# Interleaving GpSimd's minima, a new balance of two engines' accounts, and another order of the last two steps in a top-32 attention and squared-ReLU kernel

## Chip, cores and metric

The kernel runs on one core of a Trainium2 chip. The metric is device microseconds of one execution, the median over several. Before the change it is 874.69 us (three runs, 873.51 to 876.08).

The engines are named as the profile names them: PE is TensorE (PEld its weight loads), DVE is VectorE, ACT is ScalarE, POOL is GpSimd, SP is SyncE, which here only starts DMAs.

## The reference

Attention in which each row of scores keeps its 32 largest, then a two-layer network with a squared ReLU:

```python
# q, k, v: (8, 8, 576, 64) float32; w_in: (512, 2048); w_out: (2048, 512)
scores = scale * np.matmul(q, k.transpose(0, 1, 3, 2))
kth = np.partition(scores, -top_k, axis=-1)[..., -top_k:-top_k + 1]     # top_k = 32
scores = np.where(scores >= kth, scores, -1000000000.0)
attn = np.exp(scores - np.max(scores, axis=-1, keepdims=True))
attn = attn / (np.sum(attn, axis=-1, keepdims=True) + 1e-09)
x = np.matmul(attn, v).transpose(0, 2, 1, 3).reshape(4608, 512)
h = np.maximum(x @ w_in, 0.0)
out = h * h @ w_out
```

## The kernel before

**Steps.** The work is 144 steps (U), each two tiles of 128 score rows by 576 columns: 64 (batch, head) pairs, nine tiles per two heads. A step's two tiles lie side by side as `[:, 2, 576]`. The program's order is written out by hand (each instruction goes through `pin`, which keeps program order), so each engine has one queue in that order. The loop for steps 0 to 124 (Z = 125) comes first, then a second loop to step 141, then steps 142 and 143 written out, with the end of the network.

**A step's way.** For step w: `scores` (L202) has PE fill two PSUM banks sc_a and sc_b with halves of 288 columns, and ScalarE copies both into `s` (L207). `split` (L235 to 240) has VectorE take the larger of each column of one half and its partner in the other, into `tops`. `bring` (L223) has PE copy half of the tops into a free part of sc_b, called `far`. `join` (L250) has VectorE compare the two halves of tops again: the larger of each pair goes to the first 144 columns of `cat`, the smaller to the next 144. `small_mins` (L263, L264) has GpSimd put the smaller of each first pair into the last columns of cat. So cat holds the row's 576 values, sorted a little, and `topk` (L282, L286) takes 8 values from it four times, from 100, 120, 256 and 576 columns: MAX8, then MATCH_REPLACE8 to strike out what was found. The joint minima (columns 144 to 288) are first read by the third round, the small ones by the fourth.

[...]

Then `below` (L328) and `expo` (L337) have ScalarE make a mark for each score under the 32nd and the exponentials, `mask` (L333) has GpSimd combine them, `turn` (L376) transposes the weights by a DMA on SP's queue, `products` (L404) has PE multiply them by the values, `invert` (L409, L415) has VectorE take the reciprocals of the sums, and `place` (L432, L437) has ScalarE write the rows of x. A finished block of x goes through the network in pieces: `ups` (L506, with ReLU on ScalarE at L512 and the square on GpSimd at L520 or on ScalarE at L517) and `downs` (L534, out by L544 or L542).

**The accounts.** `debt` holds how far GpSimd (G) and ScalarE (A) are behind in microseconds, as the program reckons: each step takes away 5.8 and 6.0 (`pass_step`), each piece of work adds its price (`owe`). Three choices follow from it. A split is *lent* (all 288 smaller values on GpSimd, not 144) where G is under 4.9. A step is *joint* where its split is lent and G is under 4.5 (5.5 near the end): then VectorE leaves out the second operation of `join`, and GpSimd makes these minima in `joint_mins` (L256, L257). A square goes to ScalarE where A is under 5.4 and G over 5.0.

**The order around it.** In step u the small minima are those of step u + 2 (of u + 1 up to step 11), the joint ones those of u + 1, the mask is that of u - 1. GpSimd's queue in a step of the long run is:

```python
        if lead > 1:
            joint_mins(u + 1)
        if u == DEEP + 2:
            small_mins(u + 2)
        elif u != DEEP + 1:
            small_mins(u + lead)
```

and later in the step `mask(u - 1)`, with squares, casts of v (L154) and a small check (`note`) in between.

**The end.** Steps 142 and 143 fill x's last block. `x_last` (L871, L873) transposes a quarter of it on PE and copies it on ScalarE, `ups_last` (L878) multiplies that quarter by w_in into sc_a and sc_b, `square_last` (L883, L885) squares, and the last downs (L951) end the kernel. `expo_last` (L366) and `mask_last` (L371) do the last step's exponentials on ScalarE and its mask on VectorE; `turn_last` (L386 to 391) transposes on PE.

Of the kernel before, what the change touches and what calls it, by code (L numbers as in the profile page):

```python
# [22 lines left out]
def kernel(  # L23
# [34 lines left out]
    def pass_step(more=0.0):  # L58
        for e in debt:
            debt[e] = max(0.0, debt[e] - {"G": 5.8, "A": 6.0}[e] - more)  # L60

# [182 lines left out]
    def join(u):  # L244
        d = st[u]
        d["joint"] = "lent" in d and DEEP + 4 <= u < U - 6 and debt["G"] < (4.5 if u < Z + 2 else 5.5)
        if d["joint"]:
            owe(G=1.6)
        for lo, op in ((0, ALU.max), (QUAR, ALU.min))[0:1 if d["joint"] else 2]:
            pin(nc.vector.tensor_tensor(d["cat"][:, :, lo:lo + QUAR], far, d["tops"][:, :, 0:QUAR], op=op))  # L250

    def joint_mins(u):
        d = st[u]
        if d["joint"]:
            at, tops = d["cat"][:, :, QUAR:HALF].bitcast(i32), d["tops"][:, :, :].bitcast(i32)
            pin(nc.gpsimd.tensor_tensor(at, tops[:, :, 0:QUAR], tops[:, :, QUAR:HALF], op=ALU.add))  # L256
            pin(nc.gpsimd.tensor_tensor(at, at, d["cat"][:, :, 0:QUAR].bitcast(i32), op=ALU.subtract))  # L257

    def small_mins(u):
        d = st[u]  # L260
        n = HALF if "lent" in d else QUAR
        s, at = d["s"], d["cat"][:, :, HALF:HALF + n].bitcast(i32)
        pin(nc.gpsimd.tensor_tensor(at, s[:, :, 0:n].bitcast(i32), s[:, :, HALF:HALF + n].bitcast(i32), op=ALU.add))  # L263
        pin(nc.gpsimd.tensor_tensor(at, at, d["tops"][:, :, 0:n].bitcast(i32), op=ALU.subtract))  # L264

# [65 lines left out]
    def mask(u):  # L331
        w = w_two[u % 3][:, :, 0:S].bitcast(i32)
        pin(nc.gpsimd.tensor_tensor(w, w, marks[u % 2][:, :, :].bitcast(i32), op=ALU.add))  # L333

    def expo(u, x):
# [312 lines left out]
    join(0)  # L648
    small_mins(0)
    scores(1)  # L650
# [22 lines left out]
    for u in range(Z):  # L673
# [3 lines left out]
        pass_step()  # L677
        owe(A=4.5 if u < DEEP + 15 else 4.12, G=3.0)
        if u > 0:
# [21 lines left out]
        if checks:  # L701
            note()
        if lead > 1:
            joint_mins(u + 1)
        if u == DEEP + 2:
            small_mins(u + 2)
        elif u != DEEP + 1:
            small_mins(u + lead)
        dense(u, 0)
        if u and not DEEP < u < DEEP + 3:  # L710
            bring(u + lead)
        if u > 0:
            below(u - 1, 1)
            topk(u, (1,))
            if u == DEEP + 1:
                join(u + 1)
            topk(u, (2,))
            if u == DEEP + 1:
                split(u + 2)
                small_mins(u + 2)  # L720
                ahead(u + 3)
                bring(u + 2)
            topk(u, (3,))
            if u == DEEP:
                join(u + 1)
                split(u + 2)
            elif u != DEEP + 1:
                join(u + 2 if u > DEEP else u + 1)
            exps(u - 1)
            mask(u - 1)  # L730
            turn(u - 1)
# [12 lines left out]
        if u == DEEP:  # L744
            small_mins(u + 2)
            ahead(u + 3)
            bring(u + 2)
# [18 lines left out]
    for u in range(Z, U - 2):  # L766
        now[0] = u
        pass_step(0.3)
        owe(A=4.12, G=3.0)
        below(u - 1, 0)  # L770
# [9 lines left out]
        if checks:  # L780
            note()
        joint_mins(u + 1)
        small_mins(u + 2)
        if u == U - 8:
# [64 lines left out]
    topk(u, (2,), lambda: invert(u - 2))  # L849
    place(u - 2)  # L850
    topk(u, (3,))
    w = w_two[u % 3]
    for x in range(2):
        below(u, x)
        at = w[:, x, 0:S].bitcast(i32)
        pin(nc.gpsimd.tensor_tensor(at, at, marks[u % 2][:, x, :].bitcast(i32), op=ALU.add))
    turn(u)
    flush()
    square()
# [15 lines left out]
    def up_last(hp, f0, khs):  # L875
        for kh in khs:
            for n in range(4):
                pin(nc.tensor.matmul(out=hp[:, n * 128:(n + 1) * 128], lhsT=w_in[:, kh, (f0 + n) * 128:(f0 + n + 1) * 128],  # L878
                                     rhs=xl[:, kh, :], start=False, stop=(kh == KH - 2 and n == 3)))

# [16 lines left out]

    x_last((0,))
    hold["out"] = True
    u = U - 1  # L900
    topk(u, (0, 1))
    expo_last(0)
    expo_last(1)
    products(u - 2)
    downs.pop(0)()
    downs.pop(0)()
    topk(u, (2,), lambda: invert(u - 2))
    place(u - 2)
    topk(u, (3,))
    mask_last(0)  # L910
    mask_last(1)
    ups_last(one, 0)
    turn_last(0)
    ups_last(two, 0)
    x_last((1,))
    turn_last(1)
    ups_last(one, 1)
    st[u]["o"] = ps_one.tile([128, 512], f32, name="gen", bufs=2)[:, 0:130].rearrange("p (x d) -> p x d", x=2)
    products(u)
    verify(u)  # L920
    ups_last(two, 1)
    invert(u)
    place_last(u)
    note()
    downs.pop(0)()
    products(u - 1)
    x_last((3,))
    invert(u - 1)
    place(u - 1)
    downs.pop(0)()  # L930
    flush()
    pin(nc.vector.tensor_reduce(worst[:, 0:1], flags[:, :, 0:OLD], axis=mybir.AxisListType.XY, op=ALU.max))
    ups_last(one, 3)
    ups_last(two, 3)
    x_last((2,))
    sums_checked(nc.vector, OLD, 2 * U)
    pin(nc.vector.tensor_reduce(worst[:, 1:2], flags[:, :, OLD:2 * U], axis=mybir.AxisListType.XY, op=ALU.max))
    pin(nc.vector.tensor_scalar(worst[:, 0:1], worst[:, 0:1], scalar1=worst[:, 1:2], scalar2=0.0, op0=ALU.max, op1=ALU.is_gt))
    for z, bank in ((0, one), (2, two)):
        ups_last(bank, 2)  # L940
        for j in range(2):
# [143 lines left out]
```

## Time and profile before

| what | value |
|---|---|
| median of three runs | 874.69 us |
| the profiled execution | 875.31 us |
| its span on the core | 873.3 us |
| VectorE's share of busy time | 96% |
| ScalarE's | 93% |
| GpSimd's | 90% |
| TensorE's | 87% |
| granted TensorE clock, mean | 0.987 |

The span is what the profiler's records cover; 2.0 us of the execution's time lie around it. Times in rows of a timeline are from the span's start. A timeline row is: start, length, engine, line, operation, output and inputs by the program's names, count, and in brackets the idle time of the engine just before and what ended it. A row of the waits is: who waited for whom, total us, times, longest. A row of the groups is: line, engine, operation, shapes, count, then busy us and mean ns of one, then idle us before them. Rows of consecutive equal operations are merged, with their count. Ends of one operation and starts of the next overlap, so the distance between starts is the time that an operation takes of its engine.

### The profile page before, as it was taken

The numbers are of one execution on the slowest core, as the hardware profiler recorded it, in microseconds if no ns is written. First come the engines' busy times: TensorE is split into PE (matmuls) and PEld (weight loads), VectorE is DVE, ScalarE is ACT, GpSimd is POOL, SyncE is SP. The second block draws the span as 40 slices with busy tenths as digits, with TensorE's granted clock in tenths as the row PEclk, the third lists the DMA queues.
The fourth block names the chain that finished last, engine by engine and source line by source line (L and its number), as shares of the span: only waits on it lengthen the run. The fifth ranks groups of instructions, "written<-read, shape, count | busy, mean of one in ns | idle before, by whom it ended". The sixth has DMA issues, their size and how long they took to land.

```text
span 873.3 us, 19891 instructions
## 1 busy us (share of the span) xinstructions
PE 756.2 (87%) x5948; PEld 483.0 (55%) x6030; DVE 842.3 (96%) x3445; ACT 809.6 (93%) x1630; POOL 787.6 (90%) x722
## 2 busy tenths in 40 slices
PE   6998997888888988889888888898898998999976
PEld 3554555555555554555555555555655654666644
DVE  5999999999999999999999999999999999999994
ACT  2888999899999998999999999999999999999973
POOL 3688999999999999999999999999999998999751
PEclk7999999999999999999999999999999999999999
DMA  5597776545555556456655555665565555433342
GB/s 122 122 226 158 177 180 107 111 93 116 92 122 112 113 111 123 80 113 108 117 109 103 101 111 108 114 126 109 120 119 112 114 102 110 85 69 75 81 75 43
DMA packets 325442, 98.04 MB, mean 112 GB/s; under 512 B 317520, under 2 KB 317776, under 8 KB 325328
## 3 DMA queue, kind: packets, MB, share of 16 engines
q1 hardware_dynamic: 323984, 96.28, 55.5%
q8 instruction: 49, 0.80, 0.4%
q14 instruction: 65, 0.53, 0.2%
q10 hardware_dynamic: 1344, 0.43, 0.2%
HBM read 36.70 MB, written 9.44 MB: 53 GB/s over the span
## 4 chain that ended last, share of the span: by engine, by line
DVE 68%; PE 11%; issue 8%; ACT 7%; POOL 4%; DMA 1%; SPq 0%; DVEq 0%; ACTq 0%; POOLq 0%
DVE m L282 29%; DVE cat L286 21%; DVE tops L235 8%; DVE cat L250 7%; ACT s L207 2%; PE dn_ps L534 2%; PE gen L506 2%; PE sc_b L223 2%; PE sc_b L202 2%; PE av_ps L404 1%; POOL cat L263 1%; PE sc_a L202 1%; PE dn_ps L556 1%; ACT marks_a L328 1%; ACT marks_b L328 1%
## 5 line engine op out<-in xcount | busy, mean ns | idle before, releaser
L282 DVE MAX8 m<-cat 128x8 f32<-128x100 f32 (+3 forms) x1152 | 435.5, 420 | 0.0
L286 DVE MATCH_REPLACE8 cat<-m,cat 128x100 f32<-128x100 f32 (+2 forms) x864 | 259.5, 308 | 0.2
L264 POOL TENSOR_TENSOR cat<-cat,tops 128x576 int32<-128x576 int32 (+1 forms) x144 | 195.1, 1355 | 14.3 <-DVE tops L238 2.5
L263 POOL TENSOR_TENSOR cat<-s 128x576 int32<-128x576 int32 (+1 forms) x144 | 195.2, 1355 | 8.6 <-ACT s L207 7.6
L202 PE MATMUL sc_b<-qkT 64*128 64x288 f32 (+1 forms) x640 | 119.0, 452 | 44.9 <-DVE cat L250 34.5
L534 PE MATMUL dn_ps<-w_out,h 128*128 128x512 bf16 x492 | 132.9, 384 | 10.7 <-ACT wide L544 4.3
L506 PE MATMUL gen<-xT,w_in 128*128 128x256 bf16 (+1 forms) x1088 | 129.3, 265 | 1.1 <-ACT xT L466 0.7
L223 PE MATMUL sc_b<-tops,id_f 128*128 128x144 f32 x524 | 95.5, 305 | 39.5 <-ACT s L207 38.9
L506 PEld LDWEIGHTS <-w_in 128*128 128x128 bf16 x1344 | 110.2, 98 | 32.6 <-issue 19.5
L404 PEld LDWEIGHTS <-wT 128*128 128x128 bf16 (+3 forms) x1600 | 98.0, 99 | 48.1 <-issue 9.0
L223 PEld LDWEIGHTS sc_b<-tops,id_f 128*128 128x128 f32 x524 | 73.5, 190 | 80.2 <-ACT s L207 76.2
L328 ACT ACTIVATE marks_a<-s,m 128x576 bf16<-128x576 f32 x144 | 116.1, 811 | 0.0
L207 ACT ACTIVATE s<-sc_b 128x576 f32<-128x576 f32 x144 | 94.9, 659 | 18.1 <-PE sc_b L202 7.1
L202 PE MATMUL sc_a<-qkT 64*128 64x288 f32 (+1 forms) x640 | 110.9, 428 | 0.9 <-DVE tops L235 0.9
L328 ACT ACTIVATE marks_b<-s,m 128x576 bf16<-128x576 f32 x142 | 110.6, 784 | 0.0
L207 ACT ACTIVATE s<-sc_a 128x576 f32<-128x576 f32 x144 | 95.9, 666 | 6.5 <-PE sc_a L202 3.5
L235 DVE TENSOR_TENSOR tops<-sc_a,s 128x576 f32<-128x576 f32 x131 | 97.8, 747 | 0.0
L250 DVE TENSOR_TENSOR cat<-sc_b,tops 128x288 f32<-128x288 f32 x207 | 86.6, 444 | 4.6 <-PE sc_b L223 4.2
L202 PEld LDWEIGHTS sc_b<-qkT 64*128 64x128 f32 (+1 forms) x640 | 47.9, 176 | 74.1 <-DVE cat L250 45.1
L534 PEld LDWEIGHTS <-h 128*128 128x128 bf16 x560 | 48.0, 98 | 72.2 <-issue 34.4
L512 ACT ACTIVATE rl<-gen 128x512 f32<-128x512 f32 x140 | 84.0, 601 | 1.5 <-PE gen L506 1.5
L202 PEld LDWEIGHTS sc_a<-qkT 64*128 64x128 f32 (+1 forms) x640 | 55.2, 178 | 36.0 <-DVE tops L235 22.2
(133 smaller groups left out, 1348.7 us busy)
## 6 DMA issues: line engine op xcount, KB each, us to landing
out_dram<-wide SPq DMA_DIRECT2D x31, 256.0 KB, 2.6
q_raw<-in_q_dram SPq DMA_DIRECT2D x30, 256.0 KB, 3.7
k_raw<-in_k_dram SPq DMA_DIRECT2D x30, 256.0 KB, 3.8
h<-in_moe_w_in_dram SPq DMA_DIRECT2D x8, 512.0 KB, 5.1
h<-in_moe_w_out_dram SPq DMA_DIRECT2D x8, 512.0 KB, 4.4
v_raw_a<-in_v_dram SPq DMA_DIRECT2D x15, 256.0 KB, 4.0
v_raw_b<-in_v_dram SPq DMA_DIRECT2D x15, 256.0 KB, 3.9
out_dram<-wide SPq DMA_DIRECT2D x9, 128.0 KB, 2.4
```

Source lines behind the costliest of these rows:

```text
L202: pin(nc.tensor.matmul(out=sc[j][r if rest else slice(0, 128), x, 0:HALF], lhsT=qkT[r, 0, c * 128:min(S, (c + 1) * 128)], rhs=qkT[r, 1, j ...
L207: pin(nc.scalar.activation(s[:, :, j * HALF:(j + 1) * HALF], sc[j][:, :, 0:HALF], AF.Copy))
L223: pin(nc.tensor.matmul(out=far[:, x, :], lhsT=id_f[:, :], rhs=st[w]["tops"][:, x, QUAR:HALF], start=True, stop=True))
L235: pin(tt(tops[:, :, :], one, two, op=ALU.max))
L250: pin(nc.vector.tensor_tensor(d["cat"][:, :, lo:lo + QUAR], far, d["tops"][:, :, 0:QUAR], op=op))
L263: pin(nc.gpsimd.tensor_tensor(at, s[:, :, 0:n].bitcast(i32), s[:, :, HALF:HALF + n].bitcast(i32), op=ALU.add))
L264: pin(nc.gpsimd.tensor_tensor(at, at, d["tops"][:, :, 0:n].bitcast(i32), op=ALU.subtract))
L282: pin(nc.vector.max(out=m[r][:, x, :], in_=cat[:, x, at]))
L286: pin(nc.vector.match_replace(out=cat[:, x, at], in_to_replace=m[r][:, x, :], in_values=cat[:, x, at], imm_value=NEG))
L328: pin(nc.scalar.activation(marks[u % 2][:, x, :], d["s"][:, x, :], AF.Relu, bias=d["m"][3][:, x, 7:8], scale=-1.0))
L506: pin(nc.tensor.matmul(out=hp[:, n * n_rows:(n + 1) * n_rows], lhsT=w_in[:, kh, (f0 + n) * 128:(f0 + n + 1) * 128], rhs=xt(kh), start=(kh ...
L534: pin(nc.tensor.matmul(out=op[:, :], lhsT=held["h2"][:, f, c * 128:(c + 1) * 128], rhs=w_out[:, f, :], start=(f == 0), stop=(f == NF - 1)))
```

## The change

It has three parts.

1. `mins` takes the place of `small_mins` and `joint_mins` in the order. With a joint step it emits joint add, small add, joint subtract, small subtract. Without one it emits the small add and puts the subtract off (`put_off`) until just after the next `mask` (`catch_up`), in steps 0 and 1 until just after the add.
2. The accounts: 5.74 instead of 5.8 is taken off G each step, a step's own work is put down at 2.92 instead of 3.0, a joint step at 1.5 instead of 1.6, and a step is joint up to a debt of 4.9 instead of 4.5.
3. The last two steps: `place(u - 2)` of step 142 moves behind `turn(u)`; in step 143 a down piece and the products of step 141 go first, the first `x_last` later, the quarters of x in the order 0, 1, 2, 3 instead of 0, 1, 3, 2, and one reduction of the check's flags (L932) earlier.

```diff
-            debt[e] = max(0.0, debt[e] - {"G": 5.8, "A": 6.0}[e] - more)
+            debt[e] = max(0.0, debt[e] - {"G": 5.74, "A": 6.0}[e] - more)
...
-        d["joint"] = "lent" in d and DEEP + 4 <= u < U - 6 and debt["G"] < (4.5 if u < Z + 2 else 5.5)
+        d["joint"] = "lent" in d and DEEP + 4 <= u < U - 6 and debt["G"] < (4.9 if u < Z + 2 else 5.5)
         if d["joint"]:
-            owe(G=1.6)
+            owe(G=1.5)
...
+    def less(at, a, b, top):
+        add = lambda: pin(nc.gpsimd.tensor_tensor(at, a, b, op=ALU.add))
+        take = lambda: pin(nc.gpsimd.tensor_tensor(at, at, top, op=ALU.subtract))
+        return add, take
+
     def joint_mins(u):
         d = st[u]
-        if d["joint"]:
-            at, tops = d["cat"][:, :, QUAR:HALF].bitcast(i32), d["tops"][:, :, :].bitcast(i32)
-            pin(nc.gpsimd.tensor_tensor(at, tops[:, :, 0:QUAR], tops[:, :, QUAR:HALF], op=ALU.add))
-            pin(nc.gpsimd.tensor_tensor(at, at, d["cat"][:, :, 0:QUAR].bitcast(i32), op=ALU.subtract))
+        at, tops = d["cat"][:, :, QUAR:HALF].bitcast(i32), d["tops"][:, :, :].bitcast(i32)
+        return less(at, tops[:, :, 0:QUAR], tops[:, :, QUAR:HALF], d["cat"][:, :, 0:QUAR].bitcast(i32))
...
-        s, at = d["s"], d["cat"][:, :, HALF:HALF + n].bitcast(i32)
-        pin(nc.gpsimd.tensor_tensor(at, s[:, :, 0:n].bitcast(i32), s[:, :, HALF:HALF + n].bitcast(i32), op=ALU.add))
-        pin(nc.gpsimd.tensor_tensor(at, at, d["tops"][:, :, 0:n].bitcast(i32), op=ALU.subtract))
+        s, at = d["s"][:, :, :].bitcast(i32), d["cat"][:, :, HALF:HALF + n].bitcast(i32)
+        return less(at, s[:, :, 0:n], s[:, :, HALF:HALF + n], d["tops"][:, :, 0:n].bitcast(i32))
+
+    put_off = []
+
+    def catch_up():
+        while put_off:
+            put_off.pop(0)()
+
+    def mins(w):
+        add, take = small_mins(w)
+        if st[w - 1].get("joint"):
+            first, last = joint_mins(w - 1)
+            first()
+            add()
+            last()
+            take()
+        else:
+            add()
+            put_off.append(take)
...
         pin(nc.gpsimd.tensor_tensor(w, w, marks[u % 2][:, :, :].bitcast(i32), op=ALU.add))
+        catch_up()
...
-        owe(A=4.5 if u < DEEP + 15 else 4.12, G=3.0)
+        owe(A=4.5 if u < DEEP + 15 else 4.12, G=2.92)
...
-        if lead > 1:
-            joint_mins(u + 1)
         if u == DEEP + 2:
-            small_mins(u + 2)
+            mins(u + 2)
         elif u != DEEP + 1:
-            small_mins(u + lead)
+            mins(u + lead)
+        if u < 2:
+            catch_up()
...
-        owe(A=4.12, G=3.0)
+        owe(A=4.12, G=2.92)
...
-        joint_mins(u + 1)
-        small_mins(u + 2)
+        mins(u + 2)
...
     topk(u, (2,), lambda: invert(u - 2))
-    place(u - 2)
     topk(u, (3,))
...
     turn(u)
+    place(u - 2)
     flush()
...
-                                     rhs=xl[:, kh, :], start=False, stop=(kh == KH - 2 and n == 3)))
+                                     rhs=xl[:, kh, :], start=False, stop=(kh == KH - 1 and n == 3)))
...
-    x_last((0,))
     hold["out"] = True
     u = U - 1
+    downs.pop(0)()
+    products(u - 2)
     topk(u, (0, 1))
     expo_last(0)
     expo_last(1)
-    products(u - 2)
     downs.pop(0)()
-    downs.pop(0)()
+    x_last((0,))
     topk(u, (2,), lambda: invert(u - 2))
     place(u - 2)
     topk(u, (3,))
     mask_last(0)
     mask_last(1)
+    pin(nc.vector.tensor_reduce(worst[:, 0:1], flags[:, :, 0:OLD], axis=mybir.AxisListType.XY, op=ALU.max))
     ups_last(one, 0)
+    ups_last(two, 0)
     turn_last(0)
-    ups_last(two, 0)
     x_last((1,))
+    downs.pop(0)()
+    products(u - 1)
     turn_last(1)
     ups_last(one, 1)
+    invert(u - 1)
+    place(u - 1)
...
     products(u)
     verify(u)
     ups_last(two, 1)
+    x_last((2,))
     invert(u)
     place_last(u)
     note()
     downs.pop(0)()
-    products(u - 1)
     x_last((3,))
-    invert(u - 1)
-    place(u - 1)
-    downs.pop(0)()
     flush()
-    pin(nc.vector.tensor_reduce(worst[:, 0:1], flags[:, :, 0:OLD], axis=mybir.AxisListType.XY, op=ALU.max))
-    ups_last(one, 3)
-    ups_last(two, 3)
-    x_last((2,))
+    ups_last(one, 2)
+    ups_last(two, 2)
...
-        ups_last(bank, 2)
+        ups_last(bank, 3)
```

More of the change, by code (lines that the diff above doesn't have):

```diff
@@ L648 @@
     join(0)
-    small_mins(0)
+    for go in small_mins(0):
+        go()
     scores(1)
@@ L744 @@
         if u == DEEP:
-            small_mins(u + 2)
+            mins(u + 2)
             ahead(u + 3)
@@ L781 @@
             note()
-        joint_mins(u + 1)
-        small_mins(u + 2)
+        mins(u + 2)
         if u == U - 8:
```

## The prediction

> **What bounds the kernel now.** I read the page's busy shares and its chain, then windows of the steady part, then who waits for whom there.
>
> ```profile
> span 873.3 us, 19891 instructions
> PE 756.2 (87%) x5948; PEld 483.0 (55%) x6030; DVE 842.3 (96%) x3445; ACT 809.6 (93%) x1630; POOL 787.6 (90%) x722
> ...
> DVE 68%; PE 11%; issue 8%; ACT 7%; POOL 4%; DMA 1%; SPq 0%; DVEq 0%; ACTq 0%; POOLq 0%
> ```
>
> The chain runs through VectorE for 68% of the span. The windows below cover steps 28 to 123 or so; their columns are PE, PEld, DVE, ACT and POOL busy time.
>
> ```profile
> 182.00:338.00 156.00, 133.95 (x1065) 85.66 (x1075) 155.88 (x645) 150.47 (x305) 151.90 (x137) 1.00 0.56 109
> 338.00:540.00 202.00, 174.13 (x1393) 112.71 (x1412) 202.00 (x827) 200.37 (x407) 196.74 (x176) 1.00 0.57 111
> 540.00:735.00 195.00, 172.78 (x1368) 112.19 (x1384) 194.36 (x799) 192.90 (x394) 186.49 (x164) 1.00 0.59 113
> ```
>
> VectorE is busy for 202.00 of 202 us in the middle one, so time taken off it there is time off the kernel, as far as the others can follow. They stand close behind: ScalarE is busy for 200.37 us and GpSimd for 196.74. From 186 to 735 us ScalarE waits this often, and VectorE, from 100 to 735 us, once:
>
> ```profile
> ACT s L207 <- DVE cat L286: 2.3, 2, 1.3
> ACT s L207 <- DVE m L282: 1.9, 3, 1.3
> ACT s L207 <- PE sc_a L202: 1.6, 6, 0.3
> ACT qkT L138 <- PE gen L134: 1.1, 5, 0.4
> ...
> DVE cat L250 <- PE sc_b L223: 0.2, 1, 0.2
> ```
>
> ScalarE has 6.9 us of waiting in that stretch, 4.2 of it on VectorE. That is all the time by which it can follow a faster VectorE; beyond it ScalarE sets the pace.
>
> **The joint minima.** Each count here comes from adding up the two debts through the 144 steps with the listing's constants. The old ones give 81 joint steps, 131 lent splits, 95 squares on ScalarE and 45 on GpSimd, which are the counts of the rows:
>
> ```profile
> L256 POOL TENSOR_TENSOR cat<-tops 128x288 int32<-128x288 int32 x81 | 64.8, 800 | 0.0
> L257 POOL TENSOR_TENSOR cat<-cat 128x288 int32<-128x288 int32 x81 | 64.5, 796 | 6.4
> L264 POOL TENSOR_TENSOR cat<-cat,tops 128x576 int32<-128x576 int32 x131 | 184.8, 1411 | 11.0 <-DVE tops L235 0.8
> L520 POOL TENSOR_TENSOR h<-rl 128x512 bf16<-128x512 f32 x45 | 46.6, 1042 | 1.1 <-ACT rl L512 1.1
> ...
> L250 DVE TENSOR_TENSOR cat<-sc_b,tops 128x288 f32<-128x288 f32 x207 | 86.6, 444 | 4.6 <-PE sc_b L223 4.2
> L517 ACT ACTIVATE h<-rl 128x512 bf16<-128x512 f32 x95 | 60.8, 640 | 0.0
> ```
>
> The new constants give 95 joint steps (16, 30, 35, 42, 48, 51, 60, 66, 78, 88, 102, 107, 114, 119 and 122 become joint, 120 no longer is, 128 and 137 take the places of 131 and 136), the same 131 lent splits, 98 squares on ScalarE and 42 on GpSimd. So VectorE loses 14 of its 207 L250 operations, and GpSimd gains 28 operations like L256 and L257. What each takes is the distance from its start to the next one's start, since ends overlap:
>
> ```profile
> 435.60 0.80 POOL L256 TENSOR_TENSOR cat<-tops 128x288 int32<-128x288 int32 x1
> 436.48 0.80 POOL L257 TENSOR_TENSOR cat<-cat 128x288 int32<-128x288 int32 x1
> 436.61 0.80 DVE L250 TENSOR_TENSOR cat<-sc_b,tops 128x288 f32<-128x288 f32 x2
> 437.24 1.41 POOL L263 TENSOR_TENSOR cat<-s 128x576 int32<-128x576 int32 x1
> 437.33 0.75 DVE L235 TENSOR_TENSOR tops<-sc_a,s 128x576 f32<-128x576 f32 x1
> 438.72 1.41 POOL L264 TENSOR_TENSOR cat<-cat,tops 128x576 int32<-128x576 int32 x1
> 439.25 0.67 ACT L517 ACTIVATE h<-rl 128x512 bf16<-128x512 f32 x1
> 439.77 0.69 ACT L207 ACTIVATE s<-sc_b 128x576 f32<-128x576 f32 x1
> 440.09 1.41 POOL L333 TENSOR_TENSOR w_two_c<-w_two_c,marks_b 128x576 int32<-128x576 int32 x1
> ```
>
> VectorE: two L250 in 0.72 us, one is 0.36, so 14 x 0.36 = **5.0 us** off the bounding engine. This is the top of the main term.
>
> GpSimd: L256 to L257, which reads what L256 just wrote, is 0.88 us; L257 to L263, which doesn't, is 0.76. Likewise 1.48 against 1.37. So a dependent pair pays 0.12 us, and in the new order (joint add, small add, joint subtract, small subtract; or add, mask, subtract) no operation follows the one it reads. That takes 0.12 from 144 small and 81 joint pairs: 27.0 us. The 14 new joints cost 14 x 2 x 0.76 = 21.3, three fewer squares save 3 x 1.04 = 3.1. Net, GpSimd has 8.8 us less to do, and its side of the bargain holds.
>
> **What comes late by it.** In a joint step the joint subtract now stands behind the small add, 1.37 us, less the 0.12 saved. Its reader is the 256-wide MAX8 of the next step; the narrowest place is step 91:
>
> ```profile
> 531.68 0.76 PE L223 MATMUL sc_b<-tops,id_f 128*128 128x144 f32 x4 [1.41 <-ACT s L207]
> 532.81 0.45 DVE L250 TENSOR_TENSOR cat<-sc_b,tops 128x288 f32<-128x288 f32 x1
> ...
> 538.93 0.80 POOL L257 TENSOR_TENSOR cat<-cat 128x288 int32<-128x288 int32 x1
> 541.55 0.74 DVE L282 MAX8 m<-cat 128x8 f32<-128x256 f32 x2
> ```
>
> The subtract ends at 539.73, its reader starts at 541.55: 1.82 us, of which about 0.6 stay. In a step without a joint, the mask (L333) runs 1.37 + 0.12 us earlier than now, with the put-off subtract queued behind it; where ScalarE's exponentials aren't ready, GpSimd stands at the mask and everything behind it (that subtract, squares, the next adds) moves back. The subtract itself has time: its first reader is the 576-wide MAX8 two steps on (one, up to step 11). I price both waits at 0 to 0.8 us for VectorE, inside the main term.
>
> ScalarE is what I trust least. Its squares move: six go to it (steps 33, 46, 49, 50, 61, 105), three leave (82, 94, 134), at 439.77 - 439.25 = 0.52 us each. Four of them, 2.1 us, fall in steps 33 to 50. From its 6.9 us of waiting stay 4.8 for following VectorE; if the 2.7 on PE can't be squeezed, 2.1. How ScalarE holds VectorE shows in the rows above: after its copies of s, PE brings the far tops (L223, ended 532.44) and VectorE's join starts at 532.81, a margin of 0.37 us. So the main term lies between 2.1 + 0.36 (step 16, before the stretch) = 2.5 and 5.0. I take **3.3**, a third of the way up, because ScalarE in 338 to 540 us is nearer to full than to having room.
>
> **The tail.** The first x column's transposes and copy leave the head of the last step; a down piece and the products of step U-3 take their place; later ones are put in order 0, 1, 2, 3; the two placing copies of step U-4 go behind the two `below` and the transpose DMA of U-2, which starts some 0.4 us sooner on SP's queue, where nothing waits for it.
>
> ```profile
> 849.60 1.43 ACT L328 ACTIVATE marks_a<-s,m 128x576 bf16<-128x576 f32 x2
> 851.57 0.22 PE L871 MATMUL gen<-id_h,x_tok 128*128 128x128 bf16 x1 [2.25 <-ACT rl L512]
> 851.62 0.78 PE L404 MATMUL av_ps<-vau_f,wT 128*128 128x65 bf16 x10
> 851.95 2.04 POOL L520 TENSOR_TENSOR h<-rl 128x512 bf16<-128x512 f32 x2
> 852.36 1.44 ACT L366 ACTIVATE marks_b<-s,low 128x576 bf16<-128x576 f32 x2
> 852.86 0.17 DVE L409 RECIPROCAL shares<-av_ps 128x2 f32<-128x2 f32 x1 [1.97 <-PE av_ps L404]
> 854.29 1.53 DVE L371 SCALAR_TENSOR_TENSOR w_two_c<-s,m,marks_b 128x576 bf16<-128x576 f32 x2
> 862.27 0.61 PE L878 MATMUL sc_a<-xT,w_in 128*128 128x128 bf16 x8 [0.37 <-ACT xT L873]
> ```
>
> Now PE stands 2.25 us before L871 with the products (L404) queued behind it, and VectorE waits 1.97 us for these. Both waits go. But the first up product then needs the x copy that ScalarE makes after its two L366, which end at 853.80 anyway, so what is late next is ScalarE. The term lies between 0 and 1.97 + 0.37 = 2.3 us; I take **0.7**, nearer to the low end because of that ScalarE row: the 0.37 before the last ups, now covered by other ups, and some 0.3 of better order. The early `worst` reduction and the stop flags I put at nothing: the reduction runs while PE does ups; uncovered, it would cost under 1 us.
>
> A rule of the Trainium skill speaks against this part. VectorE's L371 starts 0.3 us after GpSimd's squares (L520) have ended at 853.99; moved up by VectorE's 1.97 us it would run beside them. SBUF — State Buffer, "Who interferes with whom", says that a VectorE instruction with two SBUF inputs contends with a GpSimd one that reads SBUF, and that the later one is blocked until the first is done. L371 has two such inputs. No row of this trace shows the two at once. By the rule up to one square, 1.04 us, would come back and the sum below would be some 872; by the rows it is 871.
>
> **Sum.** The profiled execution took 875.31 us, 873.3 of span and 2.0 around it: 875.31 - 3.3 - 0.7 = 871.3. It lies 0.6 above the median of the three runs, 874.69, and from that the same terms give 870.7. I forecast **871.0**.
>
> **Rivals.**
> - Full price: ScalarE and GpSimd follow all the way, the tail's waits go for half their worth: 874.7 - 5.0 - 1.0 = 868.7. For it: VectorE waits only 0.2 us in 635 now. Against it: ScalarE's 4.8 us of room must all be found where VectorE needs it.
> - Held: ScalarE's waits on PE stay, GpSimd stands at the earlier masks, and joint subtracts come late by the 0.8; the tail gives nothing: 874.7 - 2.5 + 0.8 = 873.0. For it: the margins of 0.37 and 0.6 us. Against: GpSimd has 8.8 us less work.
> - Slower, because the change doesn't do what it says: the 0.12 us belongs to the operation itself and not to reading a fresh result, so it stays. Then GpSimd has 14 x (0.88 + 0.76) - 3.1 = 19.8 us more. Its idle time in the three windows is 17.9 us, of which some 13 are such gaps (6.4/81 and 11.0/131 are 0.08 us each of idle time, in some 160 pairs), so about 5 are free; its joint subtracts then hold VectorE by about 13 us: 875.3 + 13 - 0.7 = 887. It decides where less than 15/225 = 0.07 of the 0.12 us goes. Against it: L264 followed by L333, equal work on other data, has no gap.
>
> **How the numbers follow.** Forecast 0.50, full price 0.17, held 0.23, slower 0.10. A measurement of this kernel tells about 0.3% from no change, 2.6 us, which is also the spread of the runs shown. The forecast's own range is 870 to 872.5, nearly all faster; with full price that makes 0.62 faster. Held and the forecast's edge make 0.26 within. The slower rival, and what ScalarE could lose beyond it, make 0.12. The range from 868.7 to 874.2 takes in full price and held, and leaves out the slower rival and a tail above or below.
>
> **What would show it.** Right: L250 x193, L256 and L257 x95; 0.76 and 1.37 us between starts inside the four; VectorE still above 99% in 182 to 735 us; steps without an L250 pair 0.36 shorter; no 2.25 at L871. Wrong: MAX8 of 256 waiting for GpSimd L257's successor (the joint subtract came late), L250 waiting for PE by microseconds and ScalarE without waits (ScalarE set the pace), or dependent spacing unchanged (the slower rival).

## The result, and the profile after

The changed kernel takes 879.85 us, median of 8 runs (878.02 to 882.97), against 875.25 us for the kernel before, also 8 runs, the three known before the change among them: ratio **1.0054 [1.0040, 1.0068]**, 0.54% slower. The forecast was 871.0 us, faster.

The page's head of the changed kernel, its span, busy shares and chain:

```profile
span 877.1 us, 19916 instructions
PE 761.5 (87%) x5948; PEld 482.3 (55%) x6030; DVE 839.0 (96%) x3431; ACT 811.4 (93%) x1633; POOL 795.3 (91%) x747
...
DVE 57%; issue 12%; POOL 11%; PE 10%; ACT 7%; DMA 2%; SPq 0%; POOLq 0%; ACTq 0%; DVEq 0%
```

VectorE has 3.3 us less to do and yet the span is 3.8 us longer. In the chain VectorE fell from 68% to 57% and GpSimd rose from 4% to 11%: work on GpSimd now ends some of the waits that count. The same three windows as before the change (PE, PEld, DVE, ACT, POOL):

```profile
182.00:338.00 156.00, 136.40 (x1063) 86.49 (x1078) 154.27 (x634) 151.88 (x309) 153.70 (x143) 0.99 0.60 109
338.00:540.00 202.00, 174.94 (x1390) 112.24 (x1406) 200.07 (x827) 199.81 (x407) 198.65 (x180) 1.00 0.57 109
540.00:735.00 195.00, 170.83 (x1344) 109.55 (x1362) 190.68 (x778) 190.25 (x386) 188.59 (x174) 1.00 0.58 112
```

VectorE idles 1.73, 1.93 and 4.32 us in them, where it idled 0.12, 0.00 and 0.64. Who it waits for, from 100 to 735 us (total, times, longest), where before there was a single 0.2 us:

```profile
DVE cat L306 <- POOL cat L254: 8.2, 18, 0.9
```

L306 is the strike of the rounds (the old L286: one instruction loads the eight values that were found, the next overwrites them). GpSimd makes a minimum out of an integer add and a subtract of the larger value; L253 is the add and L254 the subtract, for joint and small minima alike (the old L256, L263 and L257, L264). So VectorE, about to strike out the first eight values, stands until GpSimd has subtracted. The groups show that the kernel otherwise is what was planned:

```profile
L250 DVE TENSOR_TENSOR cat<-sc_b,tops 128x288 f32<-128x288 f32 x193 | 81.3, 442 | 3.5 <-PE sc_b L223 3.1
L306 DVE MATCH_VALUE_LOAD cat<-m,cat 128x8 f32 x864 | 68.1, 79 | 8.8 <-POOL cat L254 8.2
L253 POOL TENSOR_TENSOR cat<-tops 128x288 int32<-128x288 int32 x95 | 76.2, 802 | 0.0
L254 POOL TENSOR_TENSOR cat<-cat 128x288 int32<-128x288 int32 x95 | 76.0, 800 | 0.0
L254 POOL TENSOR_TENSOR cat<-cat,tops 128x576 int32<-128x576 int32 x131 | 185.1, 1413 | 0.0
L541 POOL TENSOR_TENSOR h<-rl 128x512 bf16<-128x512 f32 x42 | 43.5, 1044 | 0.2 <-ACT rl L533 0.2
```

There are 193 L250, 95 joint pairs and 42 squares on GpSimd, and its subtracts no longer have idle time ahead of them (6.4 and 11.0 us before).

**The place.** Step 91, the narrowest in the prediction. First the kernel before, its VectorE at the same place (the joint subtract there starts at 538.93 and ends at 539.73, a row of the prediction):

```profile
539.70 0.42 DVE L282 MAX8 m<-cat 128x8 f32<-128x100 f32 x2
540.06 0.09 DVE L286 MATCH_VALUE_LOAD cat<-m,cat 128x8 f32 x1
540.14 0.25 DVE L286 MATCH_REPLACE8 cat<-m,cat 128x100 f32<-128x100 f32 x1
```

and the changed kernel, by time over GpSimd and VectorE:

```profile
540.78 0.80 POOL L253 TENSOR_TENSOR cat<-tops 128x288 int32<-128x288 int32 x1
541.53 1.41 POOL L253 TENSOR_TENSOR cat<-s 128x576 int32<-128x576 int32 x1
542.41 0.42 DVE L302 MAX8 m<-cat 128x8 f32<-128x100 f32 x2
542.90 0.79 POOL L254 TENSOR_TENSOR cat<-cat 128x288 int32<-128x288 int32 x1
543.65 1.40 POOL L254 TENSOR_TENSOR cat<-cat,tops 128x576 int32<-128x576 int32 x1
543.72 0.09 DVE L306 MATCH_VALUE_LOAD cat<-m,cat 128x8 f32 x1 [0.89 <-POOL cat L254]
543.80 0.24 DVE L306 MATCH_REPLACE8 cat<-m,cat 128x100 f32<-128x100 f32 x1
```

The joint subtract reads the larger ones of the pairs, `cat[:, :, 0:QUAR]`, 144 wide. The first round strikes in the first 100 of these. It is a write over something still to be read, and it comes 1.49 us sooner than the reader of the subtract's result (540.06 against 541.55). Before, it had 540.06 - 539.73 = 0.33 us to spare. The new order puts the joint subtract 1.37 - 0.12 = 1.25 us later, so 0.92 of wait was to come; the row says 0.89.

**Where the difference arises.** Follow the start of each step's first MAX8 (100 wide), changed kernel minus the kernel before, each counted from its own first one: +1.0 us at step 20, +1.2 at 60, +2.4 at 80, +3.9 at 100, +5.3 at 120. The starts of step 142, the last but one, in the kernel before and then in the changed one:

```profile
842.46 0.41 DVE L282 MAX8 m<-cat 128x8 f32<-128x100 f32 x2
```

```profile
848.11 0.41 DVE L302 MAX8 m<-cat 128x8 f32<-128x100 f32 x2
```

Up to there 5.65 us were lost; the spans differ by 3.8, so the tail gave 1.85 back. Inside the loop 14 x 0.36 = 5.0 us came off VectorE (for most new joint steps, the loop step that holds the shorter join is 0.36 to 0.37 us shorter). The named waits took 8.2. What is left, some 2.5, isn't assigned to single waits.

**GpSimd** also stands more. Its largest waits from 100 to 735 us, the kernel before and then the changed one:

```profile
POOL w_two_a L333 <- ACT w_two_a L337: 2.4, 4, 0.9
POOL w_two_c L333 <- ACT w_two_c L337: 1.8, 5, 0.6
POOL h L520 <- ACT rl L512: 1.1, 1, 1.1
POOL w_two_b L333 <- ACT w_two_b L337: 0.2, 1, 0.2
```

```profile
POOL w_two_b L353 <- ACT w_two_b L358: 8.9, 7, 3.5
POOL w_two_c L353 <- ACT w_two_c L358: 5.0, 5, 1.5
POOL w_two_a L353 <- ACT w_two_a L358: 1.4, 4, 0.8
```

L353 is the mask (old L333), which now comes ahead of the put-off subtract and stands for ScalarE's exponentials: 15.3 us instead of 4.4. What is queued behind it, the next step's joint minima among it, waits with it. The order in time suggests that this is in good part an effect of the strike waits: of the 17 waits at a mask in this stretch, 11 begin 4.2 to 5.3 us after a wait at the strike, and no strike wait has a mask wait in the 6 us before it. So where VectorE was held, GpSimd later stands too, and has less time left to catch up.

### The profile page after: what moved, and what is told of

It reads as the page before. It is cut to its first block, busy times and chain, and to the rows that moved or that the text cites. A ratio compares the mean times of both kernels' runs of the same rounds, so it can differ in the third digit from the quotient of the medians.

```text
span 877.1 us, 19916 instructions
## 1 busy us (share of the span) xinstructions
PE 761.5 (87%) x5948; PEld 482.3 (55%) x6030; DVE 839.0 (96%) x3431; ACT 811.4 (93%) x1633; POOL 795.3 (91%) x747
## 4 chain that ended last, share of the span: by engine, by line
DVE 57%; issue 12%; POOL 11%; PE 10%; ACT 7%; DMA 2%; SPq 0%; POOLq 0%; ACTq 0%; DVEq 0%
DVE m L302 24%; DVE cat L306 18%; DVE tops L235 7%; DVE cat L250 5%; POOL cat L254 4%; POOL cat L253 2%; ACT s L207 2%; PE dn_ps L555 2%; POOL w_two_c L353 2%; PE gen L527 2%; PE sc_b L202 1%; PE av_ps L425 1%; PE sc_b L223 1%; POOL w_two_a L353 1%; POOL w_two_b L353 1%
## 5 line engine op out<-in xcount | busy, mean ns | idle before, releaser
L306 DVE MATCH_REPLACE8 cat<-m,cat 128x100 f32<-128x100 f32 (+2 forms) x864 | 259.3, 307 | 0.2
L253 POOL TENSOR_TENSOR cat<-s 128x576 int32<-128x576 int32 (+1 forms) x144 | 195.6, 1359 | 8.0 <-ACT s L207 7.7
L254 POOL TENSOR_TENSOR cat<-cat,tops 128x576 int32<-128x576 int32 (+1 forms) x144 | 195.4, 1357 | 0.3
L555 PE MATMUL dn_ps<-w_out,h 128*128 128x512 bf16 x492 | 133.8, 386 | 10.9 <-ACT wide L565 4.3
L202 PE MATMUL sc_a<-qkT 64*128 64x288 f32 (+1 forms) x640 | 113.1, 437 | 0.9 <-DVE tops L235 0.9
L250 DVE TENSOR_TENSOR cat<-sc_b,tops 128x288 f32<-128x288 f32 x193 | 81.3, 442 | 3.5 <-PE sc_b L223 3.1
L306 DVE MATCH_VALUE_LOAD cat<-m,cat 128x8 f32 x864 | 68.1, 79 | 8.8 <-POOL cat L254 8.2
```

What stands on the lines that cost most here:

```text
L202: pin(nc.tensor.matmul(out=sc[j][r if rest else slice(0, 128), x, 0:HALF], lhsT=qkT[r, 0, c * 128:min(S, (c + 1) * 128)], rhs=qkT[r, 1, j ...
L253: add = lambda: pin(nc.gpsimd.tensor_tensor(at, a, b, op=ALU.add))
L254: take = lambda: pin(nc.gpsimd.tensor_tensor(at, at, top, op=ALU.subtract))
L306: pin(nc.vector.match_replace(out=cat[:, x, at], in_to_replace=m[r][:, x, :], in_values=cat[:, x, at], imm_value=NEG))
L555: pin(nc.tensor.matmul(out=op[:, :], lhsT=held["h2"][:, f, c * 128:(c + 1) * 128], rhs=w_out[:, f, :], start=(f == 0), stop=(f == NF - 1)))
```

## The experiments

Three causes were possible from here: the order of the four (joint subtract too late for the strike), the put-off (GpSimd standing at the mask), and the accounts (more work on GpSimd than fits). Times are medians in us, and each ratio is to runs of the kernel before that were measured beside it. Waits are those from 100 to 735 us unless another stretch is named.

**e1: the tail alone.** The kernel before with the third part of the change only.

> The kernel before with the new order of the last two steps alone. From the two traces' step starts the changed kernel regains 1.8 us after step 143 began. If that is the tail's own worth, 1.8 us faster than before, some 873.4. If it is only slack that the late arrival left, no difference, 875.2.

873.36 against 875.41, ratio 0.9978 [0.9965, 0.9991]: 2.05 us faster. From the last step's first MAX8 to the end it takes 1.7 us less than before. The tail is a gain by itself, and the loss lies in the loop.

**e2: the accounts alone.** The constants of `owe`, `debt` and the joint's bound, with the old order.

```diff
-            debt[e] = max(0.0, debt[e] - {"G": 5.8, "A": 6.0}[e] - more)
+            debt[e] = max(0.0, debt[e] - {"G": 5.74, "A": 6.0}[e] - more)
...
-            owe(G=1.6)
+            owe(G=1.5)
```

> The kernel before in its old order with the new accounts alone: 95 joint steps, dependent pairs kept, old tail. GpSimd has 14 x 1.63 - 3 = 20 us more to do and about 5 us to spare from 100 to 735 us. If GpSimd's capacity sets what the joint steps are worth, VectorE waits for it by 10 us and more, 884 to 890. If joint steps are nearly free for GpSimd, 871 to 875.

890.27 against 875.29, ratio 1.0174 [1.0151, 1.0196], just above the 884 to 890 that were expected if GpSimd's capacity decides.

```profile
DVE cat L286 <- POOL cat L257: 16.1, 34, 1.4
```

With the 0.12 us gaps kept, 95 joints are more than GpSimd can do: it waits for others only 0.7 us in all, and the place where VectorE feels it is again the strike. The joint subtract is in its old position in the group here, so any lateness of GpSimd comes out at this point, not only one that the order makes.

**e3: the order alone.** The four interleaved and the put-off, with the old accounts and the old tail.

> The kernel before with the new order of GpSimd's minima alone: 81 joint steps, old accounts, old tail. Theory (strike): the joint subtract reads the first 144 columns of cat, which the first MATCH_REPLACE8 of the next step's topk strikes out, so that strike waits for it; put 1.25 us later it loses its margin of 0.33 us and more. Then MATCH_VALUE_LOAD waits for GpSimd by 1 to 6 us in total and the kernel is 1 to 5 us slower than before, 876 to 880. Rival (pace): the loss comes from ScalarE's extra squares and GpSimd's 28 extra operations; without them this order is neutral or better, 873 to 875.5, and MATCH_VALUE_LOAD waits stay under 0.5 us.

883.05 against 875.41, ratio 1.0082 [1.0062, 1.0102], more than was expected: the order loses by itself, with no additional joint step. But the parts don't add up. The accounts alone lose 15.0 us (e2) and the order alone 7.6, while all three parts together lose 4.6; it fits this that the order takes away the gaps with which 95 joints were too many. In e3 strikes wait, and GpSimd, with 81 joints, stands at the masks (the first rows of its waits; the profiled run was the slowest of six, 885.39):

```profile
DVE cat L306 <- POOL cat L254: 6.2, 14, 0.9
```

```profile
POOL w_two_b L353 <- ACT w_two_b L358: 12.8, 10, 1.9
POOL w_two_c L353 <- ACT w_two_c L358: 6.2, 5, 1.7
POOL w_two_a L353 <- ACT w_two_a L358: 5.4, 7, 1.6
```

**e4: the joint subtract early in its group, everything else late.** The changed kernel, with the joint pair together ahead of the small add, and the small subtract put off in every step.

```diff
             first()
-            add()
             last()
-            take()
-        else:
-            add()
-            put_off.append(take)
+        add()
+        put_off.append(take)
```

> The changed kernel, but the joint pair is emitted together ahead of the small add, as before, and the small subtract is put off behind the mask in every step. Accounts (95 joint steps) and tail as changed. Strike: the joint subtract is back at its old place, its waits fall from 8.2 to under 2 us and the time to 870.5 to 873.5. Pace: ScalarE and the early masks are as in the changed kernel, so it stays at 878 to 880.

881.45 against 875.41, ratio 1.0065 [1.0045, 1.0086]: the expectation of a gain fell. The strikes wait more than in the changed kernel, though the subtract stands sooner within its step:

```profile
DVE cat L303 <- POOL cat L254: 10.2, 19, 1.1
```

```profile
338.00:540.00 202.00, 174.78 (x1380) 111.62 (x1400) 199.12 (x822) 198.27 (x402) 199.12 (x180) 1.00 0.59 110
```

GpSimd (last of the five) is busy for 199.12 of 202 us: the joint pair has its 0.12 us back and every step's small subtract now stands behind a mask. At its masks it waits for ScalarE by only 3.6 us here, so long waits at the mask aren't needed for the loss. The place within the group isn't all either; what counts is where GpSimd stands against VectorE as the step begins. The joint add starts 1.68 us (median) ahead of its step's first MAX8 here, against 3.22 in the kernel before and 2.90 in the changed one.

**e5: the joint add a step sooner.** The changed kernel; the joint add goes out behind the mask of the step before, and the joint subtract is first in its group.

```diff
+        if "last" in st[w - 1]:
+            st[w - 1].pop("last")()
+            add()
+            put_off.append(take)
...
+    def begin(w):
+        if st[w].get("joint"):
+            first, st[w]["last"] = joint_mins(w)
+            put_off.insert(0, first)
```

> The changed kernel, but in the long loop the joint add is emitted one step sooner, right after the mask and ahead of the put-off small subtract, so that the joint subtract can be the first of the next step's minima: no operation reads the one just ahead, and the subtract comes 0.9 us sooner than even before. Strike: no wait of MATCH_VALUE_LOAD for GpSimd above 0.5 us in total, time 869.5 to 872, the best of the four. Pace: 878 to 880 as the changed kernel.

875.77 against 875.41, ratio 1.0006 [0.9993, 1.0020]: neither of the two expectations. Strike waits fall from 8.2 to 3.5 us and the loss against the kernel before is gone, but the gain isn't there, though e5 has the new tail. The small subtract still stands behind the mask, and GpSimd still waits 10.9 us in all.

**e7 and e8: the two halves of the order alone,** each on the kernel before with old accounts and old tail. e7 has the put-off and leaves the joint pair as it was; e8 interleaves the four and puts nothing off. Against the `mins` of the change, e8 differs in the branch without a joint:

```diff
-            add()
-            put_off.append(take)
+            add()
+            take()
```

> The kernel before (81 joint steps, old accounts, old tail) with one half of the new order: in steps without a joint the small subtract is put off behind the mask; joint steps as before. If the mask in front costs by itself, GpSimd waits 10 us and more at the masks from 100 to 735 us, the first strike waits by 2 to 5 us in total, 877 to 880. If only the interleaving of four does harm, no strike waits, 873 to 875.5.

> The kernel before (81 joint steps, old accounts, old tail) with the other half: the four interleaved in joint steps, nothing put off. The joint subtract ends 1.25 us later, but GpSimd has 20 us less to do and does not stand at early masks. If its place behind the small add costs by itself, strike waits of 1 to 4 us, 876 to 879. If the mask is the whole of it, no strike waits, 874 to 875.5.

e7: 878.67 against 875.29, ratio 1.0035 [1.0022, 1.0047], strike waits 2.0 us (5 times). e8: 875.54 against 875.29, ratio 0.9999 [0.9987, 1.0010], strike waits 1.3 us (3 times). The put-off costs 3.4 us alone. The interleaving costs nothing where GpSimd, freed of the gaps in its joint steps and with no more joints, has room and runs ahead. It waits 22.8 us for others there, most of it at the masks:

```profile
POOL w_two_b L353 <- ACT w_two_b L358: 10.6, 15, 1.7
POOL w_two_c L353 <- ACT w_two_c L358: 4.1, 8, 1.2
POOL w_two_a L353 <- ACT w_two_a L358: 2.4, 5, 0.8
```

These 17.1 us are more than the changed kernel's 15.3, and they cost nothing. So the sum of the waits at the mask says little; GpSimd's lead does. The room between the end of the joint subtract and the first strike, median over the joint steps, is 1.90 us in the kernel before, 1.28 in e8, 1.14 in e7, 0.61 in e3 and 0.34 in the changed kernel. In e7 the subtract has its old place in the group, so there the put-off alone has made GpSimd late by some 0.8 us. Together, in e3, the halves cost 7.6 us, more than their sum: the put-off takes GpSimd's lead, and the interleaving has taken the margin that would have covered that.

**e10: the changed kernel without the put-off.** The same edit on the changed kernel, accounts and tail kept.

> The changed kernel with its 95 joint steps and the four interleaved, but without a joint the small subtract follows its add at once and the mask comes last again. If the mask in front of the put-off subtract is what turned the gain into a loss (it alone made the kernel before 3.4 us slower), GpSimd's waits at the mask fall from 15.8 to under 8 us, strike waits from 8.2 to under 4 us and the time from 879.9 to 874 to 876.5. If the interleaving is to blame once GpSimd is loaded with 95 joint steps, it stays at 878 or more with strike waits of 6 us and more.

876.10 against 875.44, ratio 1.0004 [0.9993, 1.0015], whose interval lies clear of the change's. The change is 4.6 us above its runs of the kernel before and e10 is 0.7, so the put-off makes about 3.9 of the 4.6. Its strikes still wait, by more than the 4 us that were expected at most (the profiled run was the highest of 12, 879.22, so this is rather too much):

```profile
DVE cat L306 <- POOL cat L254: 5.1, 10, 1.0
```

Without the put-off, none of its mask waits begins within 6 us after a strike wait.

**e6: neither (the woven order).** Accounts, 95 joints and tail of the changed kernel; the joint add goes ahead by a step, the joint subtract comes first in the next, the small add and subtract have the joint add between them, nothing is put off and the mask comes last as before the change. (JOINT is the set of the same 95 steps.)

```diff
-        if st[w - 1].get("joint"):
-            first, last = joint_mins(w - 1)
+        if "last" in st[w - 1]:
+            st[w - 1].pop("last")()
+        add()
+        if w in JOINT:
+            first, st[w]["last"] = joint_mins(w)
             first()
...
+        take()
```

> The changed kernel with its 95 joint steps, accounts and tail, but another order of GpSimd's minima: joint subtract of the step before first, small add, joint add of the same step, small subtract, and the mask last, with nothing put off. Theory (strike and mask): two things made the first strike wait, the joint subtract standing 1.25 us later and the mask standing ahead of a put-off subtract, where GpSimd waits 15.8 us for ScalarE between 100 and 735 us instead of 5.5. Both are gone here, so MATCH_VALUE_LOAD waits under 1 us in total, GpSimd's waits at the mask are back under 7 us, and the time is 868.5 to 871.5. Rival (pace): 95 joint steps are more than GpSimd and ScalarE can follow in any order: 873 to 877, with VectorE waiting for GpSimd or for PE by 3 us and more.

872.73 against 875.29, ratio 0.9967 [0.9952, 0.9981]: a gain, though a smaller one than was expected. No strike waits for GpSimd, GpSimd's own waits are down to 6.4 us, and the median room ahead of the first strike is 2.45 us. e10 has the same joints, accounts and tail and puts nothing off either; it is 3.2 us slower, so with 95 joints the interleaving of four does cost something against the woven order. What VectorE waits for in e6 is the other side:

```profile
DVE cat L253 <- PE sc_b L223: 2.0, 5, 0.7
```

That is the join of the far tops (L253 here, L250 in the changed kernel), behind PE, which is behind ScalarE's copies of `s`. It is the limit on which the prediction built its main term, and it only shows once the strikes are clear.

**e11: the same order with 81 joints and the old accounts.**

> The woven order of e6 and the new tail with the 81 joint steps and accounts of before. If the 14 more joint steps are worth something once nothing waits for the strike, this is 0.5 to 3 us slower than e6, 873.2 to 875; if ScalarE's pace takes all of their 5.0 us, it is equal to e6 within 0.5 us. GpSimd has 20 us less to do than before, so no strike waits.

872.84 against 875.44, ratio 0.9975 [0.9959, 0.9991]: the same as e6. In this order the 14 additional joints, with the squares that the accounts then give (98 on ScalarE in e6, 95 here), are worth nothing in the end, and most of the 2.6 us is the tail's (e1). On the way they are worth something. From step 20 to step 80, by the starts of the steps, e6 gains 1.8 us on the kernel before and e11 gains nothing; behind step 86 e6 stops gaining and loses some of it (its profiled run was the fastest of its ten, so its trace shows rather too little of that).

**e9: 90 joints, fewer late squares for ScalarE.** e6's order and tail; the new joints only up to step 86, and after it the old set. The accounts then leave 93 squares on ScalarE and give 47 to GpSimd, the additional ones at steps 86, 100, 105, 112 and 120.

> The woven order of e6 and the new tail with 90 joint steps: the new ones up to step 86, the old ones behind it, where ScalarE was found to set the pace (in e6 VectorE's joins wait 2.0 us for PE behind ScalarE's copies, from step 88 on). By the accounts five more squares go from ScalarE to GpSimd than in e6, all behind step 86. Pace: the join waits from 100 to 735 us fall under 1 us and the time is 871 to 872.5, as good as e6 or better with five joint steps less. Rival: the late joint steps did pay, 873.5 to 875.

869.09 (868.44 to 870.04) against 875.44, ratio **0.9927 [0.9912, 0.9942]**: the fastest version, ahead of both kernels and faster than either expectation. Its last two windows:

```profile
540.00:735.00 195.00, 174.09 (x1364) 111.79 (x1381) 194.22 (x801) 192.09 (x392) 188.87 (x170) 0.99 0.59 114
735.00:842.00 107.00, 98.53 (x868) 65.80 (x881) 103.53 (x434) 98.09 (x203) 92.39 (x84) 0.98 0.38 78
```

VectorE (third) is busy for 194.22 of 195 us, and from 100 to 735 us no wait of a join for PE is listed.

**e12: e9's joints with e6's squares.** Were the fewer late joints what helped, or the squares that moved with them? The choice of each square is written out as in e6, 98 on ScalarE.

```diff
-                    if DEEP + 15 < now[0] < U - 7 and debt["A"] < 5.4 and debt["G"] > 5.0:
+                    if SQUARES.pop(0):
```

> The 90 joint steps and woven order of e9, but each square on the engine on which e6 has it: 98 on ScalarE, 42 on GpSimd, not 93 and 47. If taking five late squares (2.6 us) off ScalarE is what let VectorE keep its gain, the joins wait for PE by 1 to 2 us again from 100 to 735 us and the time is 870.5 to 872.5. If the five late joint steps less are all of it, 868.5 to 870 as e9.

872.92 against 874.98, ratio 0.9975 [0.9964, 0.9985], clear of e9's interval and near e6's 0.9967. The sign that was named for it didn't come: from 100 to 735 us its joins wait for PE by 0.3 us, once. By the starts of the steps, against the kernel before, both are 3.4 us ahead at step 100; at 120 e9 is 4.2 ahead and e12 3.0, in step 139 e9 5.0 and e12 1.8. VectorE's waits from 735 to 842 us, e12 and then e9:

```profile
DVE shares L433 <- PE av_ps L428: 2.5, 4, 1.0
DVE cat L255 <- PE sc_b L223: 2.3, 4, 0.7
```

```profile
DVE shares L431 <- PE av_ps L426: 1.6, 2, 0.9
DVE cat L253 <- PE sc_b L223: 1.0, 2, 0.7
DVE shares L431 <- ACT rl L534: 0.4, 1, 0.4
```

So it is the squares, as the two kernels differ in nothing else: e9 is 6.35 us below its runs of the kernel before and e12 2.06. Five squares are 5 x 0.52 = 2.6 us of ScalarE's time; why they are worth some 4 us, and by which waits, the traces show only in part. The woven order alone wins little (e11), more joints in it nothing (e6), and more joints with ScalarE relieved 6.35 us, some 2 of them the tail's. A kernel with 81 joints and the relieved ScalarE wasn't run, so how much of this needs the joints is open.

## Why the prediction was wrong

The step that failed is "What comes late by it": the price of 0 to 0.8 us for the late joint subtract and the mask together, put inside the main term and so at nothing in the sum. In its place the trace shows 8.2 us of waits at the strike, and the runs show 3.9 us for the put-off (e10) and 3.2 us more for the interleaving against the woven order (e10 against e6).

- **Joint subtract late.** The prediction took "its reader is the 256-wide MAX8 of the next step", with 1.82 us. The instruction that waits is the strike of the first round, which overwrites what the subtract reads, with 0.33. No MAX8 of 256 ever waits; the least room ahead of one in the changed kernel is 1.38 us. The trace of before held the warning: 19 of its 81 joint steps have under 1.25 us ahead of the strike (0.33, 0.46 and 0.59 the smallest), and what these lack sums to 7.1 us. In the changed kernel 18 waits sum to 8.2. That the two are so near is partly chance: 7.1 is a price for a GpSimd as late as before and 81 joints; where it had room (e8) 1.3 was left.
- **The mask ahead of the put-off subtract.** The text named what is queued behind the mask and then priced it at next to nothing, since the subtract itself has time. It wasn't the subtract that came late but GpSimd as a whole, and with it the next step's joint subtract: the median room ahead of the strike falls from 1.90 to 1.14 us by the put-off alone (e7). Removing the put-off gives back about 3.9 us (e10), and adding it alone costs 3.4 (e7).
- **Main term 3.3, of 5.0 at most.** The 14 L250 operations came off VectorE as worked out. That ScalarE decides how much of it can be had was right, but even 2.5 was too much for the accounts as they stand: with the strikes clear (e6 against e11) it is about 0 in the end, 1.8 us being gained up to step 80 and not kept behind it. It is kept where late squares leave ScalarE too (e9 against e12).
- **GpSimd's balance, -8.8 us.** The gaps are gone exactly: the starts of joint add and small add are 0.75 us apart and those of small add and joint subtract 1.37 (540.78, 541.53, 542.90 above). Adds and subtracts have 0.0 idle ahead of them. The balance came true: GpSimd's busy time rose by 7.7 us (787.6 to 795.3) and the idle time ahead of its subtracts fell by 17.4. But it says nothing of when the work is done, and less work didn't keep the subtracts in time.
- **The tail, 0.7 (0 to 2.3): right in sign, too small.** It gave 2.05 us in e1, whose trace has 1.7 of it in the last step, and 1.85 in the changed kernel. The row of the 0.22 us transpose that waited 2.25 us, and its products, in the changed kernel:

```profile
856.99 0.79 PE L425 MATMUL av_ps<-vau_f,wT 128*128 128x65 bf16 x10 [1.11 <-DMA wT<-w_two_a]
857.29 2.04 POOL L541 TENSOR_TENSOR h<-rl 128x512 bf16<-128x512 f32 x2
857.88 0.17 DVE L430 RECIPROCAL shares<-av_ps 128x2 f32<-128x2 f32 x1 [1.30 <-ACT low L342]
858.59 0.22 PE L892 MATMUL gen<-id_h,x_tok 128*128 128x128 bf16 x1
859.32 1.53 DVE L392 SCALAR_TENSOR_TENSOR w_two_c<-s,m,marks_b 128x576 bf16<-128x576 f32 x2
859.53 0.61 PE L899 MATMUL sc_a<-xT,w_in 128*128 128x128 bf16 x8 [0.73 <-ACT xT L894]
```

  The transpose (L892) waits for nothing and the 2.25 are gone. VectorE's 1.97 became 1.30. What ends it is two things at once: the products, which wait 1.11 for the weights that a DMA transposes and end at 857.78, and ScalarE's `low` (L342), which ends at 857.79 and is the one that the row names. That a late ScalarE comes next was right: the first up product (L899) waits 0.73 us for its x copy, where it waited 0.37. By the rule of the Trainium skill that the prediction weighed (SBUF — State Buffer, "Who interferes with whom"), L392 beside the squares would cost up to 1.04 us. In the changed kernel L392 starts at 859.32 as the squares end, at 859.33. In e6 the two do run at once:

```profile
848.64 2.04 POOL L542 TENSOR_TENSOR h<-rl 128x512 bf16<-128x512 f32 x2
850.45 1.57 DVE L393 SCALAR_TENSOR_TENSOR w_two_c<-s,m,marks_b 128x576 bf16<-128x576 f32 x2
```

  The square ends at 850.68, 0.23 us after L393 (the changed kernel's L392) starts, and the two L393 take 1.57 us instead of 1.53. It is so in e10 and e12 too (1.57 and 1.56), and 1.53 or 1.54 in all other runs. So an overlap of 0.23 us cost 0.04 us; by these rows L393 wasn't held until the square had ended, which the rule would ask for. A longer overlap was in no run, and what one would cost isn't shown.
- **Rivals.** "Held" had the right events, joint subtracts late and GpSimd standing at masks, at a tenth of their price. "Slower" priced a GpSimd with its gaps and 95 joints at 887 (its own sum, 875.3 + 13 - 0.7, gives 887.6); e2, which has both, with the old order and tail, took 890.27. But the rival was tied to the gaps staying, and those went. The side that came true, slower with the gaps gone, was in no rival.
- **What was to show it.** x193, x95 and the spacings were right. VectorE above 99% from 182 to 735 us failed: 98.9, 99.0 and 97.8% in the three windows, 98.6 over all. The sign named for a late subtract, a MAX8 of 256 that waits, couldn't have appeared.

What stays open: some 2.5 us of the loop aren't assigned to waits, how an early mask takes GpSimd's lead wasn't followed step by step, and e9's gain isn't split between joints and squares.

## What to carry to other kernels

Before an operation is moved later, look for the first instruction that touches either its result or its *operands*: an in-place step that overwrites what it reads may come well ahead of its reader, and margins to it can be read off the old trace, step by step. Their sum is a warning rather than a price: 7.1 us here, against 1.3 us of waits where the engine had room (e8) and 8.2 where it hadn't. An instruction that may have to wait for another engine, moved ahead in an in-order queue, is priced by all that is behind it and by the narrowest margin there, not by the one operation that changed places with it. Where three engines are within 3% of full, work taken off one pays as far as the next is relieved with it (e9 against e12), so move both in one step and try the halves apart. And before a wait is called a cause, see what came first in time: in the changed kernel 11 of GpSimd's 17 waits at the mask followed one of VectorE's at the strike.

## What was unexpected of the hardware

Two halves of one order cost more together than apart: +3.4 us (e7) and nothing clear of noise (e8) by themselves, +7.6 us as a pair (e3), each against its own runs of the kernel before. GpSimd's 0.12 us for reading what the operation just ahead wrote disappears entirely with one unrelated operation between: the 128x288 operation is then followed after 0.75 us, the 128x576 one after 1.37 (540.78, 541.53 and 542.90 above). And a VectorE operation with two SBUF inputs that began 0.23 us before the end of a GpSimd square took 0.04 us longer, not 0.23 (e6).
